# Two orders for the own weights at the ends of batches 2 to 6, in a block-recurrent cross attention with a SwiGLU layer behind it

## The chip, the cores and the metric

The kernel runs on one core of one Trainium2 chip. The metric is the device time of one launch in microseconds (us). The core has five engines with queues of their own: TensorE (PE in the profile, with PEld for its weight loads), VectorE (DVE), ScalarE (ACT), GpSimd (POOL) and SyncE (SP), which issues DMAs. They wait for each other only through semaphores.

## The reference

Eight batches, each with 8 heads of 512 tokens and 32 states of width 64. Tokens attend to states and states to tokens; both reads go, as 4352 rows of 512, through an RMS norm and a SwiGLU layer with 1536 hidden columns. Cut to what matters:

```python
a = softmax(scale * x @ state.T);   xread = a @ state     # 512 tokens per head
a2 = softmax(scale * state @ x.T);  sread = a2 @ x        # 32 states per head
x = concat([xread, sread], axis=2)                        # rows of H*D = 512
xn = x / sqrt(mean(x * x) + 1e-6) * rms_g
g = xn @ w_gate
out = (g * sigmoid(g) * (xn @ w_val)) @ w_out
```

## The kernel before

**How the work is tiled.** All values are float32. The tokens of a batch are never multiplied with the large weights as such. Since `xread` is `a @ state`, the states of a batch are first multiplied into the gate and value weights: the *own weights* of the batch, 256 rows (8 heads of 32 states) for each of six column groups `mp`. `own_weights(b, mp)` does that: `products` issues eight multiplications (each is two instructions in the trace, so x16) on 64 rows by 32 columns of the array (L687), into two PSUM banks `pv[0]` and `pv[1]`; `copies` moves each bank into one half of the SBUF tile `v` (L699), and `more_of_v` makes four sums of quarters of `v` (L714 to L717) into `vs` and in place. The banks come from two pools of two: `vps` (named `pv`) for `mp` 0, 2, 4 and 5, `aps` (named `at`) for `mp` 1 and 3; so own weights 0 and 2 use the same two banks, one after the other.

**The hidden layer of a batch** (`hidden_seven`) multiplies `v` and `vs` with the attention of the tokens, in seven products per `mp` instead of eight (L834, products on halves with sums, as in Strassen's scheme in Winograd's form). The first product of a batch needs the first quarter of `v` of `mp` 0, the second needs the sum of L714, the third that of L715, the fourth that of L717. Between them ScalarE copies banks out (L881, L884, L886), and VectorE adds (L897, L910). The same scheme, twice nested, makes the projection with `w_out` (`project_twice`): seven outer products of seven inner ones (L1138), with copies by ScalarE (L1151), sums by VectorE (L1178, L1186 to L1197), sums by GpSimd in `combine` (L1166 to L1171) and stores on SyncE (L1249). Its four results are `p1`, `p5`, `u2` and `c21`; `c21` is copied in two halves, and the second needs the last product.

**The next batch's start** is done beside the projection: `tokens_read` and `states_read` of batch b + 1, with the states' read itself on 128 by 32 tiles (L623), its scaling on ScalarE (L638, `sr`), a transpose (L641) and a copy (L643); the tokens' last steps are transposes (L298) and a scaling by VectorE (L442), behind which GpSimd makes sums of the attention (`slot_sums`, L752 to L755); then the own weights 0 and 1 of batch b + 1. Own weights 2 to 5 come inside the next batch.

**What sets the order.** Each stage is a Python generator that issues a few instructions per step. For every batch a string names the order in which the generators are stepped, one letter per step: `FIRST` for batch 1, `PERIOD` for batches 2 to 6, `LAST` for batch 7 (L34 to L38, L1339). Every engine, and SyncE's queue, executes its instructions in the order in which they were issued. The letters around the change: `a` tokens' read, `s` states' read, `p` a step of the projection's products, `c` a copy of its banks, `o` a store (every second step of it issues nothing), `w` `first_products` (first the sums of the attention, then the products of own weights 0, then those of 1), `x` a step of `copies` (first half, second half, sums), `f` a fetch of weights (L196), `l` a load (L134), `v` the products of own weights 2 to 5. Every `PERIOD` begins with `v` and `a`: own weights 2 and a transpose (L309) of the next but one batch's states. So at the end of a batch TensorE's instructions are: L298, L623, own weights 0, L641, the last L1138 (six instructions), own weights 1, and then, in the next string, own weights 2, L309 and the first L834.

Of the kernel before, what the change touches and what calls it, by code (L numbers as in the profile page):

```python
# [14 lines left out]
ALU = mybir.AluOpType  # L15
# [19 lines left out]
    "vahhthtxthahhhhxuutxuthahaaathatuuhluhhuhtvtvfxutuxhaxhthaghuaxhhxuauutfuxhhukkk"  # L35
    "tthhhthgauvuhtuhhkthtauhaaxaxtauhhuausufufxhutsththhaugauuthuhuughupaptuhsuuupkg"
    "kpkkpkkapppkcppkkpkppcgpppkkpkaapopkspaaapkpkkpppasacpkaaccksppkpkkpcaakspkpaaak"
    "asaappskpksspskppkaakppkgoooppppkaakappppkasoalwfswossxpxfxcwxxxcoo"  # L38
)

FIRST = (
# [19 lines left out]
def kernel(  # L61
# [21 lines left out]
    VE, SE, GE, TE = nc.vector, nc.scalar, nc.gpsimd, nc.tensor  # L83
# [47 lines left out]
    def load_x(b, *queues):  # L131
# [6 lines left out]
        for c in range(NC):  # L138
# [12 lines left out]
                     in0=ones.to_broadcast([P, NC]), op=ALU.pow)  # L151
# [6 lines left out]
    for i in range(4):  # L158
        GE.tensor_copy(groups[:, i], ident[:, 0:Ns])
        for j in range(1, 4):  # L160
            GE.tensor_tensor(out=groups[:, i], in0=groups[:, i],
                             in1=ident[:, Ns * j:Ns * j + Ns], op=ALU.add)
# [30 lines left out]
    def fetch(n):  # L193

        if NM // 2 <= n < (B + 1) * (NM // 2):
            nc.sync.dma_start(out=new_w(n), in_=w_d[n % (NM // 2)])  # L196
# [477 lines left out]
    def own_weights(b, mp):  # L674


        pv = []

        def products():
            w = w_sb.pop(b * (NM // 2) + mp)  # L680
            for e in range(2):
                pv.append(vps.tile([P, 4 * P], F32, name="pv") if b and mp in (0, 2, 4, 5) else
                          aps.tile([P, 4 * P], F32, name="at") if b or mp else
                          fx.tile([P, 4 * P], F32, name="f"))
            for j in range(4):
                for e in range(2):
                    TE.matmul(out=pv[e][Ns * j:Ns * j + Ns, :],  # L687
                              lhsT=stT_g[b][D * e:D * e + D, j, :],
                              rhs=w[D * e:D * e + D, j].rearrange("p m k f -> p (m k f)"),
                              start=True, stop=True)  # L690
            if b == 0 or b == 1 and mp < 2:
                fetch(b * (NM // 2) + mp + W_BUFS)
            yield

        def copies():
            v = (seven["v"] if b else v_0).tile([P, 2, 2, 2, P], F32, name="v")
            v_sb[b, mp] = v, None
            for e in range(2):
                SE.copy(v[:, e].rearrange("p m k f -> p (m k f)"), pv[e])  # L699
                yield  # L700
            if b:
                more_of_v(b, mp)
                yield

        return products(), copies()

    def more_of_v(b, mp):


        v, _ = v_sb[b, mp]  # L710
        vs = seven["vs"].tile([P, 3, 2, P], F32, name="vs")
        v_sb[b, mp] = v, vs
        a11, a12, a21, a22 = (v[:, e, :, k, :] for k in range(2) for e in range(2))
        GE.tensor_tensor(out=vs[:, 0], in0=a21, in1=a22, op=ALU.add)  # L714
        GE.tensor_tensor(out=vs[:, 1], in0=vs[:, 0], in1=a11, op=ALU.subtract)  # L715
        GE.tensor_tensor(out=a21, in0=a11, in1=a21, op=ALU.subtract)
        GE.tensor_tensor(out=vs[:, 2], in0=a12, in1=vs[:, 1], op=ALU.subtract)  # L717

    def hidden(m, lhs, rhs):

# [522 lines left out]
    def store_tokens(b):  # L1243
        def store(r, c0, n, ot):
            rows_ = out[T * b + P * r:T * b + S, c0:c0 + n].rearrange("(r p) f -> p r f", p=P)
            if len(ot.shape) == 2:
                nc.sync.dma_start(out=rows_[:, 0], in_=ot)
            else:
                nc.sync.dma_start(out=rows_[:, 0:2], in_=ot)  # L1249
        return store  # L1250
# [64 lines left out]
    with tc.manual_schedule(**by_hand):  # L1315
# [7 lines left out]
        for b in range(1, B):  # L1323
            h, t, u = hidden_seven(S, weights_of(b), lambda b=b: tokens_of(b), True)
            p, c, k, o = project_twice(b, store_tokens(b))
# [19 lines left out]
        p, c, k = project_seven(NT, store_states, nc.scalar)  # L1345
# [34 lines left out]
```

## Time and profile before

| what | value |
|---|---|
| time, median of 3 runs | 742.96 us (742.85 to 744.31) |
| the profiled execution: its time | 743.34 us |
| its span, first to last instruction | 741.3 us |
| granted TensorE clock over the span | 1.000 |
| TensorE busy | 733.3 us |
| VectorE busy | 555.9 us |
| ScalarE busy | 361.9 us |
| GpSimd busy | 258.6 us |

The profile comes from one execution. Its page gives busy time by engine, the chain of work that ended last, and groups of instructions by line. A row of the timeline has the start, the length, the engine, the line, the operation, the tiles (out<-in), the shape and the count of instructions merged into it; in brackets stands how long the engine was idle before it, and what ended that. A row of a group has busy us and the mean ns of one. Matmuls are pipelined, so the rows of two groups overlap by the length of one matmul, and the distance of their starts is what a group costs.

### The profile page before, as it was taken

The page shows a single profiled execution, that of the slowest core. Times are in us where ns is not written, and L with a number is a line of the kernel's source. Part 1 is how long each engine was busy: PE and PEld are TensorE (multiplying, and loading weights), DVE is VectorE, ACT ScalarE, POOL GpSimd, SP SyncE. Part 2 cuts the span into 40 slices and gives each one's busy share as a digit, 9 for nine tenths or more (in the row PEclk, how much of TensorE's full clock was granted, in tenths as well). Part 3 has the DMA queues.
Part 4 walks back from the last instruction along what each step waited for, and adds up shares of the span by engine and source line. Part 5 has one row for each costly group of instructions (what it writes and reads, how often), then busy time and mean ns, then how long its engine had stood idle before and what let it go on. Part 6 is the DMA issues. An engine that isn't in the chain of part 4 may idle for free.

```text
span 741.3 us, 14181 instructions
## 1 busy us (share of the span) xinstructions
PE 733.3 (99%) x5574; PEld 590.6 (80%) x5574; DVE 555.9 (75%) x938; ACT 361.9 (49%) x616; POOL 258.6 (35%) x362
## 2 busy tenths in 40 slices
PE   8999999999999999999999999999999999999998
PEld 6534444779977997789878997799779987899996
DVE  3877596799857994699568984799469955788862
ACT  4879742573265625473366426562557336511220
POOL 3000004341283128512662237312841267324400
PEclk9999999999999999999999999999999999999999
DMA  9978936855584288607780669338850883063311
GB/s 282 295 295 287 382 148 251 284 209 208 183 296 113 96 288 276 195 1 304 236 297 18 241 207 319 87 102 288 273 187 10 317 224 130 1 224 118 137 50 28
DMA packets 60993, 146.14 MB, mean 197 GB/s; under 512 B 14848, under 2 KB 31744, under 8 KB 54016
## 3 DMA queue, kind: packets, MB, share of 16 engines
q1 hardware_dynamic: 47808, 125.78, 48.3%
q10 hardware_dynamic: 13120, 19.47, 9.2%
q8 instruction: 44, 0.72, 0.4%
q14 instruction: 21, 0.17, 0.1%
HBM read 116.46 MB, written 28.77 MB: 196 GB/s over the span
## 4 chain that ended last, share of the span: by engine, by line
PE 98%; DVE 1%; DMA 1%; ACT 0%; SPq 0%; issue 0%
PE f L834 40%; PE f L1138 31%; PE pv L730 6%; PE f L937 6%; PE pv L687 4%; PE at L687 3%; PE f L1000 2%; PE at L623 1%; PE at L347 1%; PE at L429 1%; DMA rows<-in_state_dram 1%; PE pv L496 0%; PE at L298 0%; PE at L491 0%; PE f L1273 0%; PE f L540 0%
## 5 line engine op out<-in xcount | busy, mean ns | idle before, releaser
L834 PE MATMUL f<-aT_s,v 128*128 128x256 f32 x504 | 118.8, 381 | 0.0
L834 PEld LDWEIGHTS f<-aT_s,v 128*128 128x128 f32 x504 | 94.8, 190 | 19.4 <-DVE h L1192 4.2
L897 DVE TENSOR_TENSOR g<-g,f 128x512 f32<-128x512 f32 x84 | 55.9, 683 | 63.7 <-PE f L834 52.2
L834 PE MATMUL f<-aT_t,vs 128*128 128x256 f32 x336 | 86.8, 381 | 0.0
L1166 POOL TENSOR_TENSOR kept<-kept 128x256 f32<-128x256 f32 x28 | 20.9, 747 | 182.9 <-DVE kept L1178 101.0
L1151 ACT COPY kept<-f 128x512 f32<-128x512 f32 (+1 forms) x56 | 30.1, 538 | 105.6 <-PE f L1138 101.4
L1138 PE MATMUL f<-w,h 128*128 128x128 f32 x588 | 75.1, 277 | 0.0
L834 PEld LDWEIGHTS f<-aT_t,vs 128*128 128x128 f32 x336 | 63.0, 190 | 12.9 <-issue 3.6
L1138 PEld LDWEIGHTS f<-w,h 128*128 128x128 f32 x588 | 70.0, 192 | 1.1 <-issue 0.8
L714 POOL TENSOR_TENSOR vs<-v 128x256 f32<-128x256 f32 x42 | 31.4, 749 | 110.9 <-ACT v L699 110.6
L888 ACT ACTIVATE hb<-g 128x1024 f32<-128x1024 f32 x42 | 44.5, 1060 | 45.4 <-DVE g L897 44.5
L910 DVE TENSOR_TENSOR hb<-hb,f 128x512 f32<-128x512 f32 (+1 forms) x48 | 31.1, 648 | 28.2 <-PE f L834 28.2
L291 POOL TENSOR_TENSOR ri<-ss,mhalf 128x4 f32<-128x4 f32 (+1 forms) x9 | 8.9, 986 | 121.7 <-issue 75.2
L730 PE MATMUL pv<-aT_s,v 128*128 128x512 f32 x96 | 44.2, 598 | 0.0
L937 PE MATMUL f<-wo,hb 128*128 128x512 f32 x96 | 43.8, 598 | 0.0
L834 PE MATMUL f<-aT_t,v 128*128 128x256 f32 x168 | 43.6, 382 | 0.0
L834 PE MATMUL f<-aT_s,vs 128*128 128x256 f32 x168 | 43.3, 380 | 0.0
L1138 PE MATMUL f<-wo,h 128*128 128x128 f32 x336 | 42.1, 275 | 0.0
L1138 PE MATMUL f<-wo,hb 128*128 128x128 f32 x336 | 42.1, 275 | 0.0
L1138 PEld LDWEIGHTS f<-wo,hb 128*128 128x128 f32 x336 | 40.3, 192 | 0.4
L1138 PEld LDWEIGHTS f<-wo,h 128*128 128x128 f32 x336 | 39.8, 192 | 0.0
L910 DVE TENSOR_TENSOR hb<-hb,c 128x512 f32<-128x512 f32 (+1 forms) x48 | 34.9, 728 | 5.5 <-ACT hb L888 5.3
(225 smaller groups left out, 1590.4 us busy)
## 6 DMA issues: line engine op xcount, KB each, us to landing
w_m<-w_d SPq DMA_DIRECT2D x48, 1024.0 KB
w<-t_d SPq DMA_DIRECT2D x49, 576.0 KB
out_dram<-kept SPq DMA_DIRECT2D x28, 256.0 KB
raw<-in_moe_w_val_dram SPq DMA_DIRECT2D x6, 1024.0 KB
raw<-in_moe_w_out_dram SPq DMA_DIRECT2D x6, 1024.0 KB
w_d<-w_m SPq DMA_DIRECT2D x6, 1024.0 KB
x_b<-in_x_dram SPq DMA_DIRECT2D x6, 1024.0 KB
x_d<-xB ACTq DMA_DIRECT2D x6, 1024.0 KB
```

Source lines behind the costliest of these rows:

```text
L687: TE.matmul(out=pv[e][Ns * j:Ns * j + Ns, :], lhsT=stT_g[b][D * e:D * e + D, j, :], rhs=w[D * e:D * e + D, j].rearrange("p m k f -> p (m k ...
L714: GE.tensor_tensor(out=vs[:, 0], in0=a21, in1=a22, op=ALU.add)
L730: TE.matmul(out=to[0], lhsT=lhs(i, k), rhs=r, start=(i == 0), stop=(i == len(rhs) - 1))
L834: TE.matmul(out=ps[:, i, 0:half], lhsT=l[:, i, :], rhs=r, start=(start and i == 0 and k == 0), stop=(k == len(lhs) - 1), skip_group_check= ...
L888: SE.activation(out=hb[:, 2 * mp:2 * mp + 2, 0:n].rearrange("p m (c t) -> p m c t", c=2), in_=q["g"][:, :, :, 0:half], func=ACTF.Silu if s ...
L897: VE.tensor_tensor(out=to, in0=to, in1=q[ps][:, :, 0:half], op=ALU.add)
L910: VE.tensor_tensor(out=part, in0=part, in1=val, op=ALU.mult)
L937: TE.matmul(out=banks[r], lhsT=hb[:, m, P * r:P * r + P], rhs=wo[:, m, :], start=(m == 0), stop=(m == NM - 1))
L1000: TE.matmul(out=banks[name][:, r, :], lhsT=lhs(k)[:, P * r:P * r + P], rhs=rhs(k), start=(start and r == 0 and k == 0), stop=(k == HM - 1) ...
L1138: TE.matmul(out=to[half][:, slot, :], lhsT=lhs[:, k, :], rhs=rhs[:, k, :], start=(fresh and n in (0, 4) and k == 0), stop=(k == QM - 1), s ...
L1151: SE.copy(of_half(k, i), banks[name][i])
L1166: GE.tensor_tensor(out=k[:, 4:8:3], in0=k[:, 5:6].to_broadcast([P, 2, QD]), in1=k[:, 4:8:3], op=ALU.add)
```

## The change

The ends of batches 2 to 6 (the string `PERIOD`, so the own weights of batches 3 to 7) are put in another order. Before: own weights 0, then the transpose of the states' read, then the last product of the projection, then own weights 1. After: the last product and the first half's copy of `c21`, then the transpose and its copy, then own weights 0, then own weights 1; own weights 2 follow, as before, with the first letter of the next string. For own weights 0 of these batches (`in_row`), the copy of the second bank and the four sums move: the copy from ScalarE to VectorE, the sums from GpSimd to VectorE. One empty step of the stores and one fetch stand at other places in the string.

```diff
-    "asaappskpksspskppkaakppkgoooppppkaakappppkasoalwfswossxpxfxcwxxxcoo"
+    "asaappskpksspskppkaakppkgoooppppkaakappppkasoalwfsopcsswxxfxwxxxcoo"
...
             for e in range(2):
-                SE.copy(v[:, e].rearrange("p m k f -> p (m k f)"), pv[e])
+                (VE.tensor_copy if e and in_row(b, mp) else SE.copy)(
+                    v[:, e].rearrange("p m k f -> p (m k f)"), pv[e])
                 yield
...
+    def in_row(b, mp):
+
+        return b > 2 and mp == 0
+
     def more_of_v(b, mp):
 
 
+        E = VE if in_row(b, mp) else GE
         v, _ = v_sb[b, mp]
         vs = seven["vs"].tile([P, 3, 2, P], F32, name="vs")
         v_sb[b, mp] = v, vs
         a11, a12, a21, a22 = (v[:, e, :, k, :] for k in range(2) for e in range(2))
-        GE.tensor_tensor(out=vs[:, 0], in0=a21, in1=a22, op=ALU.add)
-        GE.tensor_tensor(out=vs[:, 1], in0=vs[:, 0], in1=a11, op=ALU.subtract)
-        GE.tensor_tensor(out=a21, in0=a11, in1=a21, op=ALU.subtract)
-        GE.tensor_tensor(out=vs[:, 2], in0=a12, in1=vs[:, 1], op=ALU.subtract)
+        E.tensor_tensor(out=vs[:, 0], in0=a21, in1=a22, op=ALU.add)
+        E.tensor_tensor(out=vs[:, 1], in0=vs[:, 0], in1=a11, op=ALU.subtract)
+        E.tensor_tensor(out=a21, in0=a11, in1=a21, op=ALU.subtract)
+        E.tensor_tensor(out=vs[:, 2], in0=a12, in1=vs[:, 1], op=ALU.subtract)
```

## The prediction

> **What bounds the kernel now.** I read the page's busy shares first, then its chain that ended last, then the waits of TensorE alone (its longest and its shortest group).
>
> ```profile
> PE 733.3 (99%) x5574; PEld 590.6 (80%) x5574; DVE 555.9 (75%) x938; ACT 361.9 (49%) x616; POOL 258.6 (35%) x362
> ...
> PE 98%; DVE 1%; DMA 1%; ACT 0%; SPq 0%; issue 0%
> ```
> ```profile
> PE f L1273 <- POOL ident masks.py:199: 1.8, 1, 1.8
> ...
> PE f L540 <- DVE eS L535: 0.3, 1, 0.3
> ```
>
> TensorE (PE) is busy for 99% of the span, the chain is PE for 98%, and no wait of PE is longer than 1.8 us. So time that another engine saves shortens nothing by itself. Two things count: how close PE's instructions stand at the five edited ends, and whether a wait comes up there. A busy row hides gaps (a matmul's own length covers the start of the next), so I read distances between starts, in PE's timeline of one end, that of batch 2:
>
> ```profile
> 283.19 0.60 PE L298 MATMUL at<-ident,ri 128*128 128x128 f32 x4
> 283.72 1.10 PE L623 MATMUL at<-x_b,e 128*32 128x64 f32 x64
> 284.75 1.09 PE L687 MATMUL pv<-w_m,stT_g 64*32 64x512 f32 x16
> 285.77 0.33 PE L641 MATMUL at<-ident,sr 128*128 128x128 f32 x1
> 285.93 0.83 PE L1138 MATMUL f<-wt,h 128*128 128x128 f32 x6
> 286.70 1.09 PE L687 MATMUL at<-w_m,stT_g 64*32 64x512 f32 x16
> 287.58 1.06 PE L687 MATMUL pv<-w_m,stT_g 64*32 64x512 f32 x16
> 288.57 0.33 PE L309 MATMUL at<-ident,rows 128*128 128x128 f32 x1
> 288.74 1.03 PE L834 MATMUL f<-aT_s,v 128*128 128x256 f32 x4
> 289.61 0.38 PE L834 MATMUL f<-aT_t,vs 128*128 128x256 f32 x1
> ```
>
> The order is: the states' read (L623), own weights 0 (L687, 284.75), a transpose (L641), the last product of the projection (L1138), own weights 1 (286.70) and 2 (287.58), a transpose (L309), the next batch's first products (L834). From L623 to L309 it is 288.57 - 283.72 = 4.85 us. The end of batch 5 measures the same, 4.86, so I price one end and multiply by five:
>
> ```profile
> 523.58 1.10 PE L623 MATMUL at<-x_b,e 128*32 128x64 f32 x64
> ...
> 528.44 0.33 PE L309 MATMUL at<-ident,rows 128*128 128x128 f32 x1
> ```
>
> Own weights followed by others take 287.58 - 286.70 = 0.88 us. Followed by full-array work (128*128 behind 64*32) they take 285.77 - 284.75 = 1.02 and 288.57 - 287.58 = 0.99. Leaving the tiled form thus costs 0.11 to 0.14, and the change takes one such exit out of each end.
>
> **PE's side.** The new order is L623, last product, L641, own 0, own 1, own 2, L309. No instruction goes or comes. Some of its distances are not shown in this stage, so I take them from others: one transpose's own length (mean, in ns), L623 followed by full-array work (batch 0), and six L1138 right behind tiled work (earlier in batch 2).
>
> ```profile
> L298 PE MATMUL at<-ident,ri 128*128 128x128 f32 x30 | 4.6, 273 | 0.0
> ```
> ```profile
> 60.13 1.10 PE L623 MATMUL at<-x_b,e 128*32 128x64 f32 x64
> 61.16 0.70 PE L730 MATMUL pv<-aT_s,v 128*128 128x512 f32 x1
> ```
> ```profile
> 270.80 0.94 PE L1138 MATMUL f<-w,hb 128*128 128x128 f32 x6
> 271.57 1.50 PE L1138 MATMUL f<-w,h 128*128 128x128 f32 x12
> ```
>
> - L623 to the last product: 61.16 - 60.13 = 1.03.
> - The last product to L641: 271.57 - 270.80 = 0.77. L641 can start at 283.72 + 1.80 = 285.52.
> - L641 to own 0: four transposes of L298 take 283.72 - 283.19 = 0.53 up to the tiled L623. Three of them at 0.11 (0.60 for four, less 0.27 for one's own length, by three) leave 0.20. Own 0 starts at T = 285.72.
> - Own 0 and own 1: 0.88 each; own 2: 0.99.
>
> The sum is 1.03 + 0.77 + 0.20 + 0.88 + 0.88 + 0.99 = 4.75, 0.10 us less per end if nothing waits.
>
> **What is late next: the banks.** ScalarE's rows of this end, and two weight loads of PE:
>
> ```profile
> 284.88 0.52 ACT L638 ACTIVATE sr<-at,z 128x64 f32<-128x64 f32 x2 [3.21 <-PE at L623]
> 286.13 0.27 ACT L643 COPY xsT<-at 128x128 f32<-128x128 f32 x1 [0.73 <-PE at L641]
> 286.30 1.08 ACT L699 COPY v<-pv 128x512 f32<-128x512 f32 x2
> ...
> 287.88 1.07 ACT L699 COPY v<-at 128x512 f32<-128x512 f32 x2
> ...
> 289.85 0.59 ACT L881 COPY g<-f 128x512 f32<-128x512 f32 x1 [0.52 <-issue]
> ```
> ```profile
> 287.43 0.31 PEld L687 LDWEIGHTS pv<-w_m,stT_g 64*32 64x32 f32 x15 [0.17 <-ACT v L699]
> 290.55 0.73 PEld L834 LDWEIGHTS f<-aT_t,vs 128*128 128x128 f32 x4 [0.32 <-issue]
> 291.44 0.73 PEld L834 LDWEIGHTS f<-aT_s,vs 128*128 128x128 f32 x4 [0.16 <-POOL vs L717]
> ```
>
> L641's input `sr` is ready at 284.88 + 0.52 = 285.40, before 285.52, so L641 needn't wait. But own 0 and own 2 share the two `pv` banks, and today 1.95 us lie between own 0 and own 1; both copies end (287.38) just ahead of own 2. In the row, own 2 wants its banks at T + 1.76. How soon a copy can be done, by ScalarE behind two own weights in a row, and by VectorE from PSUM at this size:
>
> ```profile
> 203.42 1.09 PE L687 MATMUL pv<-w_m,stT_g 64*32 64x512 f32 x16
> ...
> 204.60 0.59 ACT L699 COPY v<-pv 128x512 f32<-128x512 f32 x1 [0.52 <-PE pv L687]
> ```
> ```profile
> L493 DVE COPY xT<-at x1: 692/692/692, 11.6 to 11.6; 128x512 f32<-128x512 f32 x1
> ```
>
> A copy begins 1.18 after the group's start and takes 0.59 on ScalarE, 0.69 on VectorE. VectorE's is the later: it ends at T + 1.87. PE loads weights 0.05 after such an end (287.38 to 287.43), so own 2 starts at T + 1.92 and is held for 0.16. That is the value I take. Bounds: 0, if VectorE starts and copies faster, and 0.78, if its copy only runs behind ScalarE's (1.18 + 0.59 + 0.03 + 0.69 + 0.05 = 2.54). The Trainium skill says in "TensorEngine Tiling (Array Packing)", PSUM Bottleneck, that packing the array doesn't speed up emptying PSUM, and advises both ScalarE and VectorE for that. The rows agree: both copies in line on ScalarE (1.08) would hold own 2 until T + 2.31.
>
> **The other parts.** VectorE is free for its copy and its four sums, one sum at 0.42:
>
> ```profile
> 283.82 1.22 DVE L442 TENSOR_TENSOR aT_s<-aT_s,at 128x1024 f32<-128x1024 f32 x1 [2.02 <-PE at L298]
> 292.78 1.39 DVE L897 TENSOR_TENSOR g<-g,f 128x512 f32<-128x512 f32 x2 [7.73 <-PE f L834]
> ```
> ```profile
> L916 DVE TENSOR_TENSOR hs<-hb 128x256 f32<-128x256 f32 x3 | 1.3, 422 | 0.1
> ```
> ```profile
> 287.79 0.73 POOL L755 TENSOR_TENSOR aT_s<-aT_s 128x256 f32<-128x256 f32 x1
> ...
> 289.97 0.73 POOL L716 TENSOR_TENSOR v<-v 128x256 f32<-128x256 f32 x1
> 290.66 0.73 POOL L717 TENSOR_TENSOR vs<-v,vs 128x256 f32<-128x256 f32 x1
> ```
>
> The sums run from about T + 1.9 = 287.6 to 289.3. Today GpSimd's last (L717) ends at 291.39 and the fourth product's weights load at 291.44; without that wait it would be 290.55 + 0.87 (a product of four, 289.61 - 288.74) = 291.42. I take 0.02 off per end. The idle 0.32 ahead of 290.55 stays: the third product adds to a bank that the copy L881 reads until 290.44. ScalarE's copy of `c21`, now ahead of L643, lies in the time from 285.40 to 286.9, when ScalarE has only L643's 0.27 to do. Own 1's copies start at T + 0.88 + 1.18 = 287.78, so the first bank that L309 takes is free at about 288.4, in time. GpSimd comes to own 1's sums at about 289 instead of 291.39, and earlier to `c21` and its store: no PE wait hangs on these, so 0. SyncE's queue keeps its order of transfers; the one fetch that waits for own 0's end goes out later by at most the shift of own 0 (285.72 - 284.75 = 0.97), and nothing behind it is waited for by PE today: 0. The moved step of the stores issues nothing.
>
> **Sum.** Per end -0.10 + 0.16 - 0.02 = +0.04; five ends +0.2 us. The profiled run took 743.34 us (span 741.3), which gives 743.5 on its scale. It lies 0.38 above the median of the three runs, 742.96, and on that I forecast 743.2. About 0.2% (1.5 us, or 0.3 us per end) is what a measurement of this kernel tells from no change.
>
> **Rivals.**
>
> A. *Own 2 isn't held.* For it: VectorE behind a tiled group isn't shown, and L442 followed L298's end (283.79) within 0.03. Against: that start alone would save 0.06 of 0.16. Per end -0.12, in all -0.6: 742.4, within 0.2%.
>
> B. *VectorE's copy runs behind ScalarE's* (slower). For it: where both engines copy into one tile today, ScalarE waits for VectorE:
>
> ```profile
> 7.11 0.27 DVE L460 COPY apart<-at 64x128 f32<-64x128 f32 x1
> ...
> 7.48 0.26 ACT L461 COPY apart<-at 64x128 f32<-64x128 f32 x1 [4.15 <-DVE apart L460]
> ```
>
> Against: there both read one bank as well, here each has its own; and the product of 288.74 reads `v` before GpSimd's sum into another part of it (L716, 289.97), so parts of a tile are told apart. Price: -0.10 + 0.78 - 0.02 = +0.66 per end, +3.3: 746.3. It decides once the copy ends later than about T + 2.1 (a hold of 0.42).
>
> C. *The sums come late.* VectorE's sums read SBUF twice, beside GpSimd's slot sums (to 288.52) and own 1's sums. If each waited for a whole GpSimd operation, four would take 4 x (0.42 + 0.73) = 4.6 and end at 292.2, where 291.5 is wanted: 0.7 more per end, +3.7 in all: 746.7. Against: from 288.5 to 289 GpSimd has nothing to do, and the sums may take 0.96 each before it counts. The Trainium skill, "SBUF — State Buffer", Who interferes with whom, calls the two engines' common port pair an exclusive lock, held against GpSimd's reads by a VectorE operation with two SBUF inputs. No run here shows that pair alone; by that rule two or three of the sums would wait, and the time stays that of the forecast.
>
> D. *The change doesn't make a row that pays*: the exit saved is paid again as own 2's wait. That is the forecast itself.
>
> **Chances.** Forecast 0.66, A 0.14, B 0.10, C 0.04, and 0.06 for a gain over 0.2% that no row here gives. So faster 0.06, same 0.80, slower 0.14. The range reaches from A (742.4, less 0.3 for the scatter of the runs) to the forecast with a hold of 0.42 instead of 0.16 (+1.3: 744.5), a third of the way to B; B, C and the unexplained gain stay outside.
>
> **What would show it.** Right: L1138 directly behind L623; three L687 groups, 0.88 from the first to the second and about 1.04 from there to the third; L309 4.85 to 4.95 behind L623; no idle of the weight load behind L717. Wrong: 0.88 for the second distance (A), or about 1.6 (B); VectorE's last sum behind 291.4 (C); or a new wait of PE away from the ends.

## The result, and the profile after

The changed kernel takes 747.59 us (median of 11 runs, 745.41 to 753.06) against 742.96 (11 runs, 741.63 to 748.03). The ratio is 1.0068, with a 95% interval of 1.0039 to 1.0097. The forecast was 743.2, no change within 0.2%, with a range up to 744.5; the kernel is slower by 0.7% and lies outside it. The profiled run of the changed kernel took 752.36 us (span 750.6). It reaches the end of batch 2 4.7 us later than the run before did (288.44 against 283.72), through code that the change doesn't touch (at the first L623 it is already 64.85 against 60.13); in the other kernels below that point lies between 281.9 and 283.9. So I compare, in the profiled executions, the stretch from L623 of the end of batch 2 to the end of the span, which holds all that was changed: 741.26 - 283.72 = 457.5 us before, 750.56 - 288.44 = 462.1 after. The difference, 4.6 us, is that of the medians.

Lines behind the diff have moved by up to 6 (L834 is L840 now, L1138 is L1144, L714 is L720). The page's first part and chain, and, of TensorE's waits (in all us, times, longest), the two that are new:

```profile
PE 740.3 (99%) x5574; PEld 595.1 (79%) x5574; DVE 576.9 (77%) x963; ACT 358.7 (48%) x611; POOL 245.5 (33%) x342
...
PE 91%; DMA 6%; DVE 1%; ACT 1%; issue 0%; ACTq 0%; SPq 0%; DVEq 0%
```
```profile
PE f L840 <- ACT g L892: 1.8, 2, 1.3
...
PE pv L687 <- DMA w_m<-w_d: 0.8, 1, 0.8
```

PE is as busy as ever by its share. But the chain, 98% PE before, has 6% DMA in it, and PE waits for a copy of ScalarE (L892) and for weights (`w_m`). Neither stands at the edited place. First that place, PE's timeline of the end of batch 2:

```profile
288.44 1.10 PE L623 MATMUL at<-x_b,e 128*32 128x64 f32 x64
289.47 0.94 PE L1144 MATMUL f<-wt,h 128*128 128x128 f32 x6
290.24 0.27 PE L641 MATMUL at<-ident,sr 128*128 128x128 f32 x1
290.44 1.09 PE L687 MATMUL pv<-w_m,stT_g 64*32 64x512 f32 x16
291.32 1.06 PE L687 MATMUL at<-w_m,stT_g 64*32 64x512 f32 x16
292.26 1.30 PE L687 MATMUL pv<-w_m,stT_g 64*32 64x512 f32 x16
293.50 0.33 PE L309 MATMUL at<-ident,rows 128*128 128x128 f32 x1
```

The row is made: 1.03, 0.77, 0.20 and 0.88 as forecast. Then own 2 waits for its banks: its matmuls begin at 292.26 and last 1.30 instead of 1.06. L623 to L309 is 5.06 us, against 4.85 before.

The larger loss lies 19 us further on. SyncE's queue, ScalarE's and PE's timelines there:

```profile
299.71 0.39 SPq L1255 DMA_DIRECT2D out_dram<-kept  x1
...
301.47 0.42 SPq L196 DMA_DIRECT2D w_m<-w_d  x1
```
```profile
302.31 0.38 ACTq L332 DMA_DIRECT2D x_d<-xB  x1
...
308.99 0.60 ACT L699 COPY v<-at 128x512 f32<-128x512 f32 x1
312.76 0.31 ACTq L337 DMA_DIRECT2D xG<-x_d  x1
313.11 0.59 ACT L892 COPY g<-f 128x512 f32<-128x512 f32 x1 [3.52 <-DMA x_d<-xB]
```
```profile
311.42 1.03 PE L840 MATMUL f<-aT_s,v 128*128 128x256 f32 x4
313.75 0.92 PE L840 MATMUL f<-aT_s,v 128*128 128x256 f32 x3 [1.30 <-ACT g L892]
```

And the same rows before (SyncE, then ScalarE):

```profile
297.02 0.39 SPq L1249 DMA_DIRECT2D out_dram<-kept  x1
...
298.70 1.20 SPq L196 DMA_DIRECT2D w_m<-w_d  x1
```
```profile
297.46 0.38 ACTq L332 DMA_DIRECT2D x_d<-xB  x1
...
303.36 0.31 ACTq L337 DMA_DIRECT2D xG<-x_d  x1
```

ScalarE writes `x_d` to HBM and reads it back (L337) for the next batch's scores. The read is issued when the write has landed (in the chain the write takes from 302.31 to 312.74, the read goes out at 312.76), and what stands behind it in ScalarE's queue waits too. Before, the write was issued 1.24 us ahead of the weight fetch (1 MB, L196), and the read followed it after 5.90. Now the fetch goes first, by 0.84, and the read follows after 10.45. The copy L892, which needs nothing of `x_d`, stands behind the read; ScalarE is idle for 3.52 us ahead of it, and PE waits 1.30 us for L892. The fetch is earlier because it stands behind the store of `c21` on SyncE, and that store is 2 us earlier against the end (11.27 us behind L623 instead of 13.30), since GpSimd has lost own 0's four sums. So the traces suggest; the experiments test it.

### The profile page after: what moved, and what is told of

The parts are those of the page before. It is cut to its first block, busy times and chain, and to the rows that moved or that the text cites. A ratio compares the mean times of both kernels' runs of the same rounds, so it can differ in the third digit from the quotient of the medians.

```text
span 750.6 us, 14200 instructions
## 1 busy us (share of the span) xinstructions
PE 740.3 (99%) x5574; PEld 595.1 (79%) x5574; DVE 576.9 (77%) x963; ACT 358.7 (48%) x611; POOL 245.5 (33%) x342
## 4 chain that ended last, share of the span: by engine, by line
PE 91%; DMA 6%; DVE 1%; ACT 1%; issue 0%; ACTq 0%; SPq 0%; DVEq 0%
PE f L840 34%; PE f L1144 31%; PE pv L736 6%; PE f L943 6%; DMA x_d<-xB 4%; PE pv L687 3%; PE f L1006 2%; PE at L687 2%; DMA w_m<-w_d 1%; PE at L623 1%; PE at L347 1%; PE at L429 1%; PE pv L496 1%; PE f L1279 1%; DVE xB L330 1%; DMA rows<-in_state_dram 1%
## 5 line engine op out<-in xcount | busy, mean ns | idle before, releaser
L840 PE MATMUL f<-aT_s,v 128*128 128x256 f32 x504 | 119.6, 382 | 1.9 <-ACT g L892 1.8
L840 PEld LDWEIGHTS f<-aT_s,v 128*128 128x128 f32 x504 | 94.5, 190 | 22.3 <-DVE h L1198 4.2
L840 PE MATMUL f<-aT_t,vs 128*128 128x256 f32 x336 | 86.5, 382 | 0.0
L1144 PE MATMUL f<-w,h 128*128 128x128 f32 x588 | 75.1, 277 | 0.0
L840 PEld LDWEIGHTS f<-aT_t,vs 128*128 128x128 f32 x336 | 63.0, 190 | 12.7 <-issue 1.4
L720 POOL TENSOR_TENSOR vs<-v 128x256 f32<-128x256 f32 x37 | 28.7, 777 | 128.9 <-ACT v L699 128.8
L1144 PEld LDWEIGHTS f<-w,h 128*128 128x128 f32 x588 | 70.0, 192 | 1.2 <-issue 0.8
L840 PE MATMUL f<-aT_t,v 128*128 128x256 f32 x168 | 43.7, 382 | 0.0
L840 PE MATMUL f<-aT_s,vs 128*128 128x256 f32 x168 | 43.1, 379 | 0.0
L1144 PE MATMUL f<-wo,h 128*128 128x128 f32 x336 | 42.1, 275 | 0.0
L1144 PE MATMUL f<-wo,hb 128*128 128x128 f32 x336 | 42.1, 275 | 0.0
L1144 PEld LDWEIGHTS f<-wo,hb 128*128 128x128 f32 x336 | 40.3, 192 | 0.4
L892 ACT COPY g<-f 128x512 f32<-128x512 f32 x42 | 24.9, 593 | 32.5 <-PE f L840 26.3
```

What stands on the lines that cost most here:

```text
L840: TE.matmul(out=ps[:, i, 0:half], lhsT=l[:, i, :], rhs=r, start=(start and i == 0 and k == 0), stop=(k == len(lhs) - 1), skip_group_check= ...
L892: SE.copy(gates(q)[1], q["x"][:, :, 0:half])
L1144: TE.matmul(out=to[half][:, slot, :], lhsT=lhs[:, k, :], rhs=rhs[:, k, :], start=(fresh and n in (0, 4) and k == 0), stop=(k == QM - 1), s ...
```

## The experiments

**Theory 1 (transfer):** the moved sums bring the fetch ahead of the write of `x_d`; that makes the most of the loss. **Theory 2 (ends):** the loss is at the five ends, in the hold of own 2, and the late transfers go along with it. Later a third came in for what was left: **late fetch**, at the end of batch 6.

All kernels in one table. "Write to read" is the time from the issue of `x_d`'s write to the first read, in the batches 3 to 6; "stretch" is L623 of the end of batch 2 to the end of the span, "last part" the same from the end of batch 6. These three columns come from one profiled execution of each kernel, the medians and ratios from 10 to 12 runs. The ratios of e1 to e4 are against 742.92 us for the kernel before, those of e5 to e7 against 742.74.

| kernel | median us | ratio to before (95%) | L623 to L309 | write to read | last part | stretch |
|---|---|---|---|---|---|---|
| before | 742.96 | | 4.86 | 5.9, 5.9, 5.9, 6.0 | 137.7 | 457.5 |
| after | 747.59 | 1.0068 (1.0039 to 1.0097) | 5.06 | 10.4, 9.6, 9.2, 8.3 | 139.0 | 462.1 |
| e1, sums on GpSimd | 745.20 | 1.0023 (1.0006 to 1.0040) | 5.06 | 5.9, 5.9, 5.9, 8.5 | 139.1 | 459.7 |
| e2, fetch behind the write | 744.29 | 1.0017 (0.9996 to 1.0038) | 5.06 | 5.8, 5.8, 5.8, 5.8 | 138.7 | 459.1 |
| e3, sums alone, old order | 744.43 | 1.0021 (1.0002 to 1.0040) | 4.86 | 9.4, 9.8, 10.4, 8.8 | 137.6 | 460.1 |
| e4, other banks | 746.43 | 1.0039 (1.0020 to 1.0058) | 4.74 | 9.5, 9.4, 9.1, 9.7 | 139.1 | 460.4 |
| e5, e2 and the old end of 6 | 743.46 | 1.0004 (0.9990 to 1.0017) | 5.06 | 5.8, 5.8, 5.8, 5.8 | 137.7 | 458.1 |
| e6, e5 and other banks | 741.39 | 0.9975 (0.9958 to 0.9992) | 4.74 | 5.8, 5.8, 5.8, 5.8 | 137.7 | 456.8 |
| e7, order alone | 746.10 | 1.0036 (1.0014 to 1.0058) | 5.33 | 5.9, 5.9, 5.9, 9.6 | 138.7 | 461.1 |

**e1: own 0's sums back on GpSimd**, all else as changed.

```diff
-        E = VE if in_row(b, mp) else GE
+        E = GE
```

> The changed kernel with own 0's four sums given back to GpSimd (order and VectorE's copy stay). Theory 1 (transfer): the sums' leaving GpSimd brought the store of c21 and the weight fetch behind it on SyncE 2 us forward, ahead of the write of x_d, whose landing then came 8.3 to 10.4 us after its issue instead of 5.9, with ScalarE's queue and so PE standing; so x_d is back at 5.9 and from the end of batch 2 (L623) to the last instruction it is 462.1 - 2.7 = 459.4 us instead of 462.1 (before: 457.5), a time near 744.9. Theory 2 (ends): the loss is in the five ends, where own 2 is held by VectorE's copy; these stay (5.06 us from L623 to L309 against 4.85), so 462 and a time near 747.6.

The stretch is 459.7, the time 745.20 (theory 1 said 459.4 and 744.9), while the ends stay at 5.06. Three of the four writes are back at 5.9. The fourth is not, and it shows how narrow the matter is. SyncE's and ScalarE's rows of batch 6 in e1:

```profile
537.88 0.42 SPq L196 DMA_DIRECT2D w_m<-w_d  x1
```
```profile
538.02 0.38 ACTq L332 DMA_DIRECT2D x_d<-xB  x1
...
546.52 0.31 ACTq L337 DMA_DIRECT2D xG<-x_d  x1
```

The fetch is 0.14 us ahead, and the read comes 8.50 behind the write. Before, in the same batch, the fetch was 0.04 behind (537.36 against 537.32), and it was 5.96:

```profile
537.36 2.26 SPq L196 DMA_DIRECT2D w_m<-w_d  x1
```
```profile
537.32 0.43 ACTq L332 DMA_DIRECT2D x_d<-xB  x1
...
543.28 0.31 ACTq L337 DMA_DIRECT2D xG<-x_d  x1
```

The packets show what lies between. In the profile q1 carries SyncE's transfers and q10 ScalarE's: the four fetches of 1 MB that e2, below, moves to ScalarE's queue are 4.2 MB less on q1 and as much more on q10. These are the packets (count, MB, share) from 1 to 4 us behind the write's issue, first before, then in e1:

```profile
q10 hardware_dynamic: 481, 0.99, 92.3%
q1 hardware_dynamic: 117, 0.10, 12.1%
```
```profile
q1 hardware_dynamic: 110, 0.63, 96.4%
q10 hardware_dynamic: 8, 0.02, 1.4%
```

Before, the write moves 0.99 MB in these 3 us and SyncE's queue 0.10; in e1 the write moves 0.02 and SyncE's queue 0.63. So they hardly share: the one that was issued first moves, and the other mostly stands. And while the fetch moves, less moves in all: 0.65 MB in 3 us, against 1.09.

**e2: the fetch behind the write.** The sums stay on VectorE and the store stays early; only the first fetch of batches 3 to 6 goes out on ScalarE's queue, behind the write.

```diff
-            fetch(n)
+            fetch(n, nc.scalar if n == first and 2 < b < B - 1 else nc.sync)
```

> The changed kernel with the first weight fetch of batches 3 to 6 issued on ScalarE's queue right behind the write of x_d (sums stay on VectorE, the store of c21 stays early). Theory 1 (transfer): the write of x_d has the DMA engines to itself again, lands 5.9 to 6.5 us after its issue, and from the end of batch 2 to the last instruction it is about 459.4 us, a time near 744.9. Theory 2 (ends): no change against the changed kernel, 462 and 747.6.

```profile
294.50 0.39 SPq L1255 DMA_DIRECT2D out_dram<-kept  x1
```
```profile
297.08 0.38 ACTq L332 DMA_DIRECT2D x_d<-xB  x1
...
300.94 0.35 ACTq L196 DMA_DIRECT2D w_m<-w_d  x1
...
302.90 0.32 ACTq L337 DMA_DIRECT2D xG<-x_d  x1
```

The store is as early as in the changed kernel (2.58 us ahead of the write), and the read follows the write after 5.82. The stretch is 459.1. The four periods from end to end are 80.10 us each, where the changed kernel has 81.66, 80.88, 80.43 and 80.15. So it is the place of the fetch, not that of the store or of the sums, that costs. (On ScalarE's queue the fetch starts 3.86 us behind the write, not 1.24 as before; e1 shows the same cure with the fetch left on SyncE.)

**e3: the sums alone, in the old order.** The kernel before, with own 0's four sums of batches 3 to 7 on VectorE and nothing else.

```diff
+        E = VE if b > 2 and mp == 0 else GE
...
-        GE.tensor_tensor(out=vs[:, 0], in0=a21, in1=a22, op=ALU.add)
+        E.tensor_tensor(out=vs[:, 0], in0=a21, in1=a22, op=ALU.add)
```

> The kernel before with nothing but own 0's four sums of batches 3 to 7 moved from GpSimd to VectorE; order and copies as before. Theory 1 (transfer): ends stay at 4.85 us, but the store of c21 and the fetch go out about 2 us earlier and x_d lands 8 to 10 us after its issue: 457.5 + 2.7 = 460.2 us from the end of batch 2 to the last instruction, a time near 745.7. Theory 2 (ends): with the old order own 2 isn't held, so 457.5 and 743.0 or a little less.

```profile
294.72 0.42 SPq L196 DMA_DIRECT2D w_m<-w_d  x1
```
```profile
295.54 0.38 ACTq L332 DMA_DIRECT2D x_d<-xB  x1
...
304.90 0.31 ACTq L337 DMA_DIRECT2D xG<-x_d  x1
305.25 0.59 ACT L887 COPY g<-f 128x512 f32<-128x512 f32 x1 [2.42 <-DMA x_d<-xB]
```

The ends are 4.86, the fetch is 0.82 ahead of the write, and the stretch is 460.1: the loss of 2.6 us comes without any row. Theory 2 would have had 457.5; it falls as the explanation of the most. The time, 744.43, lies 1.5 us above that of the kernel before, not 2.6, and below the 745.7 that was expected; the interval of its ratio, 0.15 to 3.0 us, holds both, and I don't know a reason for the rest.

**e4: other banks for own 0.** What the hold of own 2 itself costs.

```diff
-                pv.append(vps.tile([P, 4 * P], F32, name="pv") if b and mp in (0, 2, 4, 5) else
+                pv.append((fy, fz)[e].tile([P, 4 * P], F32, name="f") if in_row(b, mp) else
+                          vps.tile([P, 4 * P], F32, name="pv") if b and mp in (0, 2, 4, 5) else
```

> The changed kernel with own 0 of batches 3 to 7 in the two banks fy and fz, so that own 2 needn't wait for own 0's copies. Theory 1 (transfer): L623 to L309 goes from 5.06 to about 4.75 us, five times -0.3 = -1.5, and x_d stays late: 460.6 us from the end of batch 2 to the last instruction, a time near 746.1. Theory 2 (ends): the loss is gone with the hold: 457 and a time of 742.5 to 743.

```profile
283.63 1.10 PE L623 MATMUL at<-x_b,e 128*32 128x64 f32 x64
284.66 0.94 PE L1145 MATMUL f<-wt,h 128*128 128x128 f32 x6
285.43 0.27 PE L641 MATMUL at<-ident,sr 128*128 128x128 f32 x1
285.63 1.09 PE L688 MATMUL f<-w_m,stT_g 64*32 64x512 f32 x16
286.52 1.06 PE L688 MATMUL at<-w_m,stT_g 64*32 64x512 f32 x16
287.38 1.06 PE L688 MATMUL pv<-w_m,stT_g 64*32 64x512 f32 x16
288.37 0.33 PE L309 MATMUL at<-ident,rows 128*128 128x128 f32 x1
```

Without the hold L623 to L309 is 4.74 us; the forecast sum without waits was 4.75. The stretch falls by 1.7 to 460.4 (theory 1 said 460.6), with the writes still late.

**e5: e2, and the old end of batch 6.** In e2 the periods between ends are 80.1 us against 79.96 before, and 0.97 is left in the last part (138.69 against 137.72).

```diff
-        return b > 2 and mp == 0
+        return 2 < b < 7 and mp == 0
...
+PERIOD_6 = PERIOD[:-67] + "asaappskpksspskppkaakppkgoooppppkaakappppkasoalwfswossxpxfxcwxxxcoo"
...
-            for stream in FIRST if b == 1 else LAST if b + 1 == B else PERIOD:
+            for stream in FIRST if b == 1 else LAST if b + 1 == B else PERIOD_6 if b + 2 == B else PERIOD:
```

> The kernel with the first fetch behind the write of x_d (e2), and the end of batch 6 in the old order with own 0 of batch 7 copied by ScalarE and summed by GpSimd. Theory (late fetch): what remains in e2 is the end of batch 6, where own 0's later end delays the fetch into its buffer by 0.9 us and batch 7 reads own 4 some 8 us later, so PE waits; then the stretch from L623 of the end of batch 6 to the last instruction goes from 138.7 to 137.7 us, and from the end of batch 2 on it is 458.1 us (e2: 459.1, before: 457.5), a time near 743.4. Rival (the hold of own 2 alone, 0.16 per end): the stretch loses only 0.16, 458.9, a time near 744.1.

The last part is back at 137.7, the stretch 458.1, as the late fetch has it. The rows of the changed kernel (SyncE, then PE) show the wait, and those before show it absent:

```profile
614.78 1.55 SPq L196 DMA_DIRECT2D w_m<-w_d  x2
```
```profile
623.01 1.09 PE L687 MATMUL at<-w_m,stT_g 64*32 64x512 f32 x16
624.92 1.14 PE L687 MATMUL pv<-w_m,stT_g 64*32 64x512 f32 x10 [0.82 <-DMA w_m<-w_d]
```
```profile
605.85 2.56 SPq L196 DMA_DIRECT2D w_m<-w_d  x2
```
```profile
615.78 1.06 PE L687 MATMUL pv<-w_m,stT_g 64*32 64x512 f32 x16
```

Batch 7 has its own order and reads own 3 and 4 sooner: 8 to 9 us behind their fetches, not 15 as in batches 3 to 6. Own 3's fetch, which waits for own 0's end, went out 3.22 us behind L623 (at 611.56) instead of 2.31 (at 603.54). Own 4's followed it by 0.86 us instead of 1.89, so it was itself no later behind L623 (4.08 against 4.20). But it landed 9.14 us after its issue, and PE, which came to own 4 after 8.46 us, waited 0.82. Before, PE came after 8.04 us and didn't wait. e5 changes the whole end of batch 6, so it shows the place; that it is this fetch is read from the row of the wait, not shown by itself.

**e6: all three repairs** (e5 with e4's banks).

> All three repairs together: own 0 of batches 3 to 6 in the banks fy and fz, the first fetch behind the write of x_d, the end of batch 6 in the old order. Theory (transfers and the hold are all that cost): four ends of 4.74 us from L623 to L309 instead of 4.86, the fourth product 0.16 us sooner, x_d at 5.8, so 457.5 - 4 x 0.16 = 456.9 us from the end of batch 2 on, and a time near 742.3, 0.1% below the kernel before. Rival (something in the row still costs): 457.5 or more, 743 or more.

741.39 us, ratio 0.9975 (0.9958 to 0.9992): the row, with its side effects taken away, is faster than the kernel before. By the traces it gains 457.5 - 456.8 = 0.7 us, four periods of 79.78 us instead of 79.96 (0.16 each was expected); the medians of the runs differ by 1.35, against 742.74 for the kernel before. No run has the other banks without the new order, so the share of the order alone in this gain isn't shown. PE's only waits are again the four of the first batch, 0.3 to 1.8 us.

**e7: the order alone**, with both copies on ScalarE and the sums on GpSimd.

> The new order alone: own 0's copies both by ScalarE, its sums by GpSimd, as before. Theory (the banks set the row): ScalarE's second copy ends about 0.26 us later than VectorE's did, own 2 waits for it, L623 to L309 takes 5.3 us instead of 5.06, and from the end of batch 2 on it is e1's 459.7 + 5 x 0.26 = 461.0 us, a time near 746.5. Rival (VectorE's copy gains nothing, the hold is that of the first bank): 5.06 and 459.7, a time near 745.2.

L623 to L309 is 5.33 and the stretch 461.1. So VectorE's copy does shorten the hold, by 0.27 per end against e1. That the stretch meets the expected 461.0 so well is in part chance: the first three periods are 0.26 longer than in e1, as expected, but the fourth is 0.97 longer, since the write to read in batch 6 is 9.6 there (the fetch is 0.44 us ahead of the write, in e1 0.14), and the last part is 0.38 shorter.

## Why the prediction was wrong

- **PE's side was right.** 1.03, 0.77, 0.20, 0.88, 0.88 and 0.99 were read off other places and came out; e4 measured 4.74 for the 4.75.
- **The hold of own 2 was right in kind, and sized too small.** Forecast 0.16; measured (292.26 and 1.30 against 1.06) it moves L309 by 0.32 (5.06 against e4's 4.74). The hold isn't where the forecast had it: own 2 begins only 0.06 late, since its first bank is free with ScalarE's copy (292.21), but its second instruction, which goes to the other bank, comes at 292.48, 0.06 behind the end of VectorE's copy (292.42). And that copy started 1.29 behind own 0, not 1.18:

```profile
291.62 0.59 ACT L699 COPY v<-pv 128x512 f32<-128x512 f32 x1 [0.81 <-PE pv L687]
291.73 0.69 DVE L699 COPY v<-pv 128x512 f32<-128x512 f32 x1 [1.97 <-POOL aT_t L759]
```

  The row names GpSimd's L759, which ended just then. But in e1 the copy starts the same 1.29 behind own 0 (285.68), and its row names own 0. What VectorE has ahead of each of the five copies is a waiting instruction of its own, in the changed kernel as in e1:

```profile
286.97 0.69 DVE L699 COPY v<-pv 128x512 f32<-128x512 f32 x1 [1.97 <-PE pv L687]
```
```profile
L699 DVEq EVENT_SEMAPHORE  x5: 21/21/21, 291.7 to 614.8; - x5
```

  ScalarE's copy beside it has none. That this costs the 0.11 isn't tested. It is 0.11 of the 0.16 that were missing; the other 0.05 isn't traced. The term for the fourth product, -0.02, was too small in its turn: with e2's periods of 80.10 against 79.96, an end costs 0.14 us, 0.07 less than the 0.21 that L623 to L309 grew; in e1, with the sums on GpSimd, it is only 0.02 less (80.15 for a period). The sum said 0.04; five ends make 0.7 us of the 4.6.
- **The step that failed** is the sentence on GpSimd and SyncE: that own 1's sums, `c21` and its store come earlier, "no PE wait hangs on these, so 0". An earlier transfer was priced as harmless. SyncE's queue did keep its order, as the prediction says; but the order between two queues changed, for the fetch got ahead of a write on which ScalarE's queue stands. By e2 this is worth 2.7 us (the periods of the changed kernel, 81.66, 80.88, 80.43 and 80.15, less 80.10 each), by e3 2.6. It is also the prediction's own last sign of being wrong, "a new wait of PE away from the ends".
- **The 0 for the fetch behind own 0's end failed too**, at one end of five. The shift was as forecast (0.91 us, at most 0.97), but "nothing behind it is waited for by PE today" says nothing on how much room there is. In batches 3 to 6 PE comes to own 3 and 4 some 15 us behind their fetches, in batch 7 after 8 to 9. That is 0.8 to 1.1 us (e2's and the changed kernel's last part, less the end's own 0.14).
- **Rivals.** A and B didn't happen: own 2 was held, and VectorE's copy (291.73) ran beside ScalarE's (291.62). C, the late sums, came half true: three of the four sums took 0.94 to 0.98 instead of 0.42, just the 0.96 that was named as the bound, and the last ended at 295.70 while the fourth product came at 296.4. None of the rivals had the loss; the 0.14 for slower stood on mechanisms that didn't happen.

The three terms, 2.7, 0.7 and 1.1, make 4.5 of the 4.6 us.

## What to carry to other kernels

When work leaves an engine, follow what that engine issues or releases later, into the DMA queues, up to the next transfer that somebody stands behind: earlier can be worse. A wait that doesn't exist today is no proof of slack; for each transfer that moves, look up which one it passes. And where a row of work is closed up, give its members their own banks first: here the order paid only when own 2 no longer waited for own 0's copies.

## What the runs showed of the hardware

The order of issue of two transfers of 1 MB, on two queues, decides sharply which moves first. With the fetch 0.04 us behind, the write was read back after 5.96 us and moved 0.99 MB between 1 and 4 us behind its issue; with the fetch 0.14 ahead, it was read back after 8.50 and moved 0.02 MB. In the batches 3 to 6 of all nine kernels, every write with the fetch ahead was read back after 8.3 to 10.5 us, and every one with the fetch behind after 5.8 to 6.0. How much later it gets isn't told by the lead: in batch 3 a fetch 0.84 ahead gave 10.45 in the changed kernel, one 0.82 ahead 9.36 in e3. What else decides that is open.

This kernel has room for about 8.9 us from write to read, an estimate from these periods: with 8.3 (the changed kernel) and 8.8 (e3) they stayed as they were, 9.2 cost 0.3 us and 10.4 cost 1.5.

VectorE's sums beside GpSimd's, in the changed kernel:

```profile
292.49 0.74 POOL L761 TENSOR_TENSOR aT_s<-aT_s 128x256 f32<-128x256 f32 x1
292.53 0.98 DVE L720 TENSOR_TENSOR vs<-v 128x256 f32<-128x256 f32 x1
293.55 0.43 DVE L721 TENSOR_TENSOR vs<-vs,v 128x256 f32<-128x256 f32 x1
```

The first sum starts 0.04 behind a GpSimd operation and takes 0.98. The second, with GpSimd idle at its start, takes 0.43. This agrees with the exclusive lock of the Trainium skill's "SBUF — State Buffer", Who interferes with whom. The wait is a little shorter than the whole GpSimd operation, though: 0.70 of it was left, and 0.70 + 0.42 would be 1.12.

With both copies on ScalarE (e7) the end took 5.33 us, with one on VectorE (e1) 5.06. This bears out the advice of the Trainium skill's "TensorEngine Tiling (Array Packing)", PSUM Bottleneck, to empty PSUM with both engines.
